# A subtraction on [128, 1024] tiles moved from VectorE to GpSimd

## The chip, the cores and the metric

The kernel runs on one core of one Trainium2 chip. The metric is the device time of one execution in microseconds (us): the median of three runs. A profiled execution stands beside them; its span is the time from the first to the last instruction, and its own time is a little longer than the span.

## The reference

The kernel computes a pooled attention followed by a two-layer block.

```
a      = softmax(phi over the 576 rows)            # 32 memory slots per head
k_m    = a^T k ;  v_m = a^T v                      # 8 batches x 8 heads, 64 wide
attn   = softmax(q k_m^T / 8) ;  out = attn v_m
x      = out, heads side by side                   # 4608 x 512
h      = x @ w_in                                  # 512 x 2048
g      = h - tanh(h)
result = g @ w_out                                 # 2048 x 512, float32
```

The weights arrive as float64.

## The kernel before

Every factor of the two large products is held as two float16 halves, a high half and the remainder (the low half), and three matmuls (high x high, high x low, low x high) stand in for one float32 matmul. The weights become win_hi, win_lo, wout_hi and wout_lo; the attention rows become ah and al; and the product of v_m and w_in becomes ph and pl, so that h comes straight from the attention weights.

The 4608 rows are cut into 18 units of 256, and the 2048 columns of w_in into 4 blocks of 512. A piece of work is a pair (unit, block), written (u, fb), and there are 72 of them. For each pair:

- mm1 (L444): TensorE computes h, four tiles of 128 columns side by side, [128, 1024] float32 in PSUM, from ph, pl, ah and al. ScalarE squares it (L450).
- g1: VectorE multiplies h with its square (L458) into h3, and frees h in PSUM; ScalarE squares u + beta (L459).
- g2: VectorE finishes the value, a polynomial for h - tanh(h), in h3 (L464); ScalarE copies it as float16 into gg[:, 0], the high half (L466).
- g3 (L471): the low half, gg[:, 1] = h3 - gg[:, 0], [128, 1024], float32 minus float16, written as float16. In two of the 72 pairs the difference is made by TensorE and ScalarE instead (L477 to L479).
- mm2 (L498): 24 matmuls with 512 columns add the pair into the two output tiles of its unit. For each output tile eight of them take the high half and four the low half. Where the pair is the last of its sum, the order is high and low of the first output tile, then of the second, so the first low matmul is the ninth; elsewhere both high parts come first, and the first low matmul is the seventeenth.

The tile h3 has two buffers, u two and gg three; h in PSUM has two.

The order of work is in two parts. The first is a list of words written by hand (START), in which all engines get their instructions in the order of the list: the words H, a, b, c and M followed by unit and block stand for mm1, g1, g2, g3 and mm2. It covers units 0 to 3 and the first half of unit 4, and between these words are the loads, the attention of the first batches, and the conversion of the weights from float64. The conversion is done by VectorE with whole-number instructions on [128, 512] (L260, L264, L268), followed by the low half of the weights (L295). The units 0 to 3 are summed in two passes, blocks 0 and 1, then 2 and 3; the partial results go to memory and back, and these DMAs, and the output of those units, are issued by GpSimd (L522). All others are issued by SyncE.

The second part is a regular loop over the rest, one pair to a slot. mm2 of a pair is issued two slots after its mm1. The attention of the batches to come is put between the slots; with it VectorE makes pl from PSUM (L423), transposes scores (L196) and takes maxima, sums and products over them (L205 to L222), and makes al (L399).

Of the kernel before, what the change touches and what calls it, by code (L numbers as in the profile page):

```python
# [14 lines left out]
ALU = mybir.AluOpType  # L15
# [209 lines left out]
def split_path(ctx, tc, c, ins, out):  # L225
    nc = tc.nc
# [241 lines left out]

    def g3(u, fb):
        h3, gg = gs[u, fb]  # L470
        nc.vector.tensor_tensor(gg[:, 1], h3, gg[:, 0], op=ALU.subtract)  # L471

    def g3_pe(u, fb):
        h3, gg = gs[u, fb]
# [52 lines left out]
    def warm(*_):  # L527
# [12 lines left out]
        "N": lambda b: att.norm(b, st[b]), "U": lambda b: att.turn(b, st[b]), "UV": att_turn_v, "W": att_window,  # L540
        "S": lambda b, t: att.scores(b, st[b], t), "A": lambda b, i, j: att.soft1(b, st[b], i, j), "B": lambda b, i, j: att.soft2(b, st[b], i, j), "BH": att_ah, "BL": att_al,
        "Z": warm, "P": att_p, "PL": att_pl, "H": mm1, "a": g1, "b": g2, "c": g3, "d": g3_pe,
        "T": lambda x, y: conv(10 * x + y, False), "E": lambda x, y: conv(10 * x + y, True),
        "L": lambda x, y: low_dve(10 * x + y), "K": lambda x, y: low_pe(10 * x + y),
# [41 lines left out]
    for sl, (u, fb) in enumerate(slots, 18):  # L586
        for f in (mm1, g1, g2, g3):
            f(u, fb)
        queue.append((u, fb))
        for f, x in tasks.get(sl, []):  # L590
            f(x)
        u, fb = queue.pop(0)
        mm2(u, fb, fb == (2 if u in parts else 0), fb == NFB - 1)
        if sl == 68:
            check(tc, c, big, ps_a)
# [210 lines left out]
```

## Time and profile before

| what | value |
|---|---|
| median of three runs | 696.86 us (695.42 to 697.27) |
| profiled execution: its time | 696.4 us |
| profiled execution: span | 694.6 us |
| PE busy | 664.5 us, 96% |
| DVE (VectorE) busy | 477.4 us, 69% |
| ACT (ScalarE) busy | 398.3 us, 57% |
| POOL (GpSimd) busy | 10.8 us, 2% |
| chain that ended last, by engine | PE 78%, DVE 17%, DMA 3%, issue 1%, ACT 1% |
| mean granted clock of TensorE | 0.991 |

In the profile PE is TensorE's matmuls, PEld its weight loads, SP SyncE's queue. L471 is line 471 of the kernel. A row of groups has the line, the engine, the operation, what it writes and reads, the count, then the busy time, the mean duration of one in ns, and the idle time of the engine just before, with what ended it. A row of the timeline has the start, the duration (of all that are merged in the row), and the instruction. A row of the waits says who waited for whom, the total, how often, and the longest. The chain is followed back from the last instruction; its rows have a start, a length, and who held it. A matmul's end is modelled, so what PE really waits for is read from the waits and the chain, not from the busy share.

### The profile page before, as it was taken

What the parts mean: (1) busy time and instruction counts of PE and PEld (TensorE: products, weight loads), DVE (VectorE), ACT (ScalarE), POOL (GpSimd) and SP (SyncE); (2) the same over time, 40 slices, a digit from 0 to 9 for tenths busy, and PEclk for the clock granted to TensorE, in tenths of its full rate; (3) what the DMA queues carried; (4) which work ended last, traced back from release to release, by engine and by line L of the source; (5) the groups of instructions that cost most, each with busy time, mean ns of one, the idle gap of its engine ahead of it and who ended that gap; (6) DMA issues with size and microseconds to landing.
All of it is one profiled execution on the core that took longest, in us unless ns stands there. A gap on an engine that the chain in (4) does not pass through costs nothing.

```text
span 694.6 us, 13671 instructions
## 1 busy us (share of the span) xinstructions
PE 664.5 (96%) x5992; PEld 392.1 (56%) x5992; DVE 477.4 (69%) x571; ACT 398.3 (57%) x526; POOL 10.8 (2%) x26
## 2 busy tenths in 40 slices
PE   2688999999999999999999999999999999999996
PEld 2345574664656556666555655665566555666552
DVE  6699999998976596446596559556955695444541
ACT  3447666664545865665865595556645664544341
POOL 0000000001000000000000000000000000000000
PEclk9799999999999999999999999999999999999999
DMA  9955534682413940002940195009200300000001
GB/s 322 361 200 202 194 130 156 205 278 77 148 62 108 341 130 6 27 16 89 344 131 2 59 361 157 2 32 331 96 1 31 123 32 1 32 1 32 1 30 36
DMA packets 34003, 84.87 MB, mean 122 GB/s; under 512 B 3472, under 2 KB 8208, under 8 KB 33936
## 3 DMA queue, kind: packets, MB, share of 16 engines
q1 hardware_dynamic: 32512, 79.59, 33.3%
q0 software_dynamic: 1280, 4.20, 1.6%
q8 instruction: 49, 0.80, 0.5%
q14 instruction: 18, 0.15, 0.1%
q10 hardware_dynamic: 144, 0.13, 0.1%
HBM read 72.37 MB, written 11.53 MB: 121 GB/s over the span
## 4 chain that ended last, share of the span: by engine, by line
PE 78%; DVE 17%; DMA 3%; issue 1%; ACT 1%; SPq 0%; DVEq 0%
PE o L498 47%; PE h L444 22%; PE pkv L147 3%; PE pp L411 3%; DVE wt L264 2%; DVE wt L268 2%; DVE h L458 2%; DVE h L464 2%; DVE wt L260 1%; DMA kv<-in_kva_dram 1%; PE psc L187 1%; DVE g L471 1%; DVE ph L423 1%; DVE wout_lo L295 1%; DMA chk<-in_w_out_dram 1%
## 5 line engine op out<-in xcount | busy, mean ns | idle before, releaser
L498 PE MATMUL o<-wout_hi,g 128*128 128x512 f16 x1152 | 354.4, 379 | 0.8 <-ACT g L466 0.8
L498 PEld LDWEIGHTS <-g 128*128 128x128 f16 x1728 | 164.2, 98 | 206.9 <-issue 16.7
L498 PE MATMUL o<-wout_lo,g 128*128 128x512 f16 x576 | 218.4, 379 | 0.0
L444 PE MATMUL h<-ah,ph 128*128 128x256 f16 (+3 forms) x1536 | 201.2, 246 | 0.4 <-DVE h L458 0.4
L444 PEld LDWEIGHTS <-ph 128*128 128x128 f16 x2304 | 178.6, 98 | 28.9 <-issue 2.5
L444 PE MATMUL h<-al,ph 128*128 128x256 f16 (+3 forms) x768 | 170.1, 246 | 0.0
L458 DVE SCALAR_TENSOR_TENSOR h<-h,u 128x1024 f32<-128x1024 f32 x72 | 87.5, 1218 | 67.6 <-ACT u L450 67.6
L450 ACT ACTIVATE u<-h 128x1024 f32<-128x1024 f32 x72 | 73.2, 1018 | 91.5 <-PE h L444 91.5
L471 DVE TENSOR_TENSOR g<-h,g 128x1024 f16<-128x1024 f32 x70 | 85.3, 1221 | 49.8 <-ACT g L466 49.8
L466 ACT ACTIVATE g<-h 128x1024 f16<-128x1024 f32 x72 | 76.0, 1056 | 72.9 <-DVE h L464 72.9
L459 ACT ACTIVATE u<-u,beta 128x1024 f32<-128x1024 f32 x72 | 82.6, 1147 | 51.3 <-DVE h L458 50.6
L464 DVE SCALAR_TENSOR_TENSOR h<-u,h 128x1024 f32<-128x1024 f32 x72 | 87.9, 1221 | 25.8 <-ACT u L459 24.5
L423 DVE SCALAR_TENSOR_TENSOR ph<-pp,ph 128x1024 f16<-128x1024 f32 x32 | 38.9, 1216 | 2.4 <-ACT ph L418 2.4
L418 ACT ACTIVATE ph<-pp 128x1024 f16<-128x1024 f32 x32 | 32.5, 1016 | 1.9 <-PE pp L411 1.9
L516 ACT ACTIVATE ot<-o 128x512 f32<-128x512 f32 x35 | 20.5, 588 | 14.3 <-PE o L498 14.2
L147 PE MATMUL pkv<-kv,e 128*32 128x129 f32 (+1 forms) x640 | 25.6, 294 | 2.6 <-DMA kv<-in_kva_dram 2.2
L196 DVE STREAM_TRANSPOSE sc<-psc 128x288 f32<-128x288 f32 x32 | 13.5, 459 | 19.6 <-PE psc L187 19.6
L309 ACT ACTIVATE fy<-chk 128x512 f32<-128x512 f32 x32 | 21.4, 667 | 5.2 <-DMA chk<-in_w_in_dram 2.8
L310 ACT ACTIVATE fy<-fy,one 128x512 f32<-128x512 f32 x32 | 23.0, 719 | 0.7
L147 PEld LDWEIGHTS pkv<-kv,e 128*32 128x32 f32 (+1 forms) x640 | 17.1, 114 | 10.8 <-issue 5.9
L264 DVE SCALAR_TENSOR_TENSOR wt<-raw,wt 128x512 uint32<-128x512 uint32 x32 | 20.7, 688 | 0.0
L268 DVE SCALAR_TENSOR_TENSOR wt<-raw,wt 128x512 uint32<-128x512 uint32 x32 | 20.6, 687 | 0.0
(96 smaller groups left out, 372.3 us busy)
## 6 DMA issues: line engine op xcount, KB each, us to landing
kv<-in_kva_dram SPq DMA_DIRECT2D x32, 516.0 KB, 7.7
q<-in_qt_dram SPq DMA_DIRECT2D x16, 576.0 KB, 7.0
raw<-in_w_in_dram SPq DMA_DIRECT2D x16, 512.0 KB, 6.6
raw<-in_w_out_dram SPq DMA_DIRECT2D x16, 512.0 KB, 5.1
chk<-in_w_in_dram SPq DMA_DIRECT2D x16, 512.0 KB, 5.0
chk<-in_w_out_dram SPq DMA_DIRECT2D x16, 512.0 KB, 5.3
out_dram<-ot SPq DMA_DIRECT2D x27, 256.0 KB, 2.0
pt<-in_phx_dram SPq DMA_DIRECT2D x8, 576.0 KB, 4.4
```

Of the source, the lines that this page charges most:

```text
L147: nc.tensor.matmul(pa[32 * h : 32 * h + 32, r, 0:129], e[0:K, c, 32 * hh : 32 * hh + 32], d["kv"][h][0:K, r, c, :], start=(c == 0), stop=( ...
L264: nc.vector.scalar_tensor_tensor(t, r[:, :, 0], 29, t, op0=ALU.logical_shift_right, op1=ALU.bitwise_or)
L268: nc.vector.scalar_tensor_tensor(t, r[:, :, 1], 0xC0000000, t, op0=ALU.bitwise_and, op1=ALU.bitwise_or)
L423: nc.vector.scalar_tensor_tensor(pl, pa, S_P / (S_V * S_W), ph, op0=ALU.mult, op1=ALU.subtract)
L444: nc.tensor.matmul(hp[:, k, tu : tu + w], px[:, g, cs], d[ax][:, g, ta : ta + w], start=(n == 0), stop=(n == 5),)
L450: nc.scalar.activation(uu, hp, AF.Square, scale=1.0 / (S_A * S_P))
L458: nc.vector.scalar_tensor_tensor(h3, hp, C2 * S_G / (S_A * S_P), uu, op0=ALU.mult, op1=ALU.mult)
L459: nc.scalar.activation(uu, uu, AF.Square, bias=c["beta"])
L464: nc.vector.scalar_tensor_tensor(h3, uu, CC, h3, op0=ALU.add, op1=ALU.mult)
L466: nc.scalar.activation(gg[:, 0], h3, AF.Copy)
L471: nc.vector.tensor_tensor(gg[:, 1], h3, gg[:, 0], op=ALU.subtract)
L498: nc.tensor.matmul(o, gx[:, k, P * tt : P * tt + P], wx[:, 4 * fb + k, :], start=(first and k == 0 and wx is wout_hi and gx is gh), stop=( ...
```

## The change

The subtraction g3 is issued on GpSimd's queue instead of VectorE's. Nothing else in the source is changed; g3 is called 70 times, 16 of them for units 0 to 3 and the first two of unit 4 through the word c, the rest from the loop.

```diff
     def g3(u, fb):
         h3, gg = gs[u, fb]
-        nc.vector.tensor_tensor(gg[:, 1], h3, gg[:, 0], op=ALU.subtract)
+        nc.gpsimd.tensor_tensor(gg[:, 1], h3, gg[:, 0], op=ALU.subtract)
```

On GpSimd's queue, in the hand-ordered part, the subtractions stand between the DMA issues of the partial results. Before (d is a partial result in memory, ot the tile it comes from):

```order
L522 DMA d_808<-ot_806 128x512
L522 DMA d_824<-ot_822 128x512
L522 DMA d_1055<-ot_1053 128x512
L522 DMA d_1071<-ot_1069 128x512
L522 DMA d_1248<-ot_1246 128x512
L522 DMA d_1264<-ot_1262 128x512
```

and now (g_747 belongs to the pair (0,1), g_914 to (1,1), g_1079 to (2,0), g_1092 to (2,1), g_1227 to (3,0), g_1370 to (3,1)):

```order
L471 TENSOR_TENSOR g_747<-h_705,g_747 128x1024
L522 DMA d_808<-ot_806 128x512
L522 DMA d_824<-ot_822 128x512
L471 TENSOR_TENSOR g_914<-h_898,g_914 128x1024
L522 DMA d_1055<-ot_1053 128x512
L522 DMA d_1071<-ot_1069 128x512
L471 TENSOR_TENSOR g_1079<-h_1038,g_1079 128x1024
L471 TENSOR_TENSOR g_1092<-h_1073,g_1092 128x1024
L522 DMA d_1248<-ot_1246 128x512
L522 DMA d_1264<-ot_1262 128x512
L471 TENSOR_TENSOR g_1227<-h_1180,g_1227 128x1024
L471 TENSOR_TENSOR g_1370<-h_1307,g_1370 128x1024
```

The subtraction of (3,0) is behind the two issues of d_1248 and d_1264, each of which waits for ScalarE's output copy.

On VectorE, in the middle of the same part, two subtractions leave a row of instructions that convert weights (wt, win_lo) and finish the pairs (2,0), (2,1) and begin (3,0):

```order
 L295 SCALAR_TENSOR_TENSOR win_lo<-wt_1081,win_hi 128x512
 L295 SCALAR_TENSOR_TENSOR win_lo<-wt_1082,win_hi 128x512
-L471 TENSOR_TENSOR g_1079<-h_1038,g_1079 128x1024
-L471 TENSOR_TENSOR g_1092<-h_1073,g_1092 128x1024
 L458 SCALAR_TENSOR_TENSOR h_1180<-h_1123,u_1148 128x1024
 L260 TENSOR_SCALAR wt_1187<-raw_1150 128x512
```

L458 of (3,0), which writes the h3 buffer that (2,0) had, now follows the weights' low half directly, and has a wait on GpSimd that it did not need while the subtraction was ahead of it on VectorE's own queue.

## The prediction

> **What bounds the kernel now.** I read the windows first, because a busy share over the whole span mixes two stages.
>
> ```profile
> 75.00:155.00 80.00, 79.08 (x750) 48.19 (x748) 79.76 (x111) 50.43 (x67) 5.53 (x8) 1.00 0.59 196
> 155.00:170.00 15.00, 15.00 (x102) 6.27 (x102) 13.52 (x18) 6.92 (x8) 1.08 (x2) 1.00 0.24 80
> 260.00:680.00 420.00, 419.73 (x3754) 250.61 (x3753) 253.09 (x257) 246.27 (x318) 0.00 (x0) 1.00 0.23 80
> ```
>
> The columns after the length are PE, weight loads, DVE, ACT and POOL busy, then the granted clock and the DMA share. From 260 to 680 us PE is busy 419.73 of 420 us at full clock while DVE works 253 us: TensorE is the bound. From 75 to 155 us (the hand-ordered start, from the first subtraction on) DVE is busy 79.76 of 80 us and PE 79.08: both are full. Next, who keeps PE waiting from 75 us on:
>
> ```profile
> PE o L498 <- ACT g L466: 0.8, 1, 0.8
> PE psc L187 <- DVE sc L196: 0.3, 1, 0.3
> PE pp L411 <- DVE e L135: 0.2, 1, 0.2
> ```
>
> That is all: 1.3 us by this table, 1.2 us by the windows (0.92 + 0.27). **So the largest possible gain is 1.2 us**, however much VectorE is relieved; a loss has no such limit. The chain of waits says where a late VectorE would hurt:
>
> ```profile
> 152.62 1.15 DVE h L464
> 153.78 1.07 ACT g L466
> 154.90 5.35 PE o L498 x24
> ```
>
> Ahead of these rows the chain runs through DVE for the whole of the full window, and only here does it pass to PE, where it stays. The second matmul of (0,3) starts as soon as its high half exists. Whatever VectorE loses between 75 and 154 us, PE loses there.
>
> **What is moved.** 70 subtractions:
>
> ```profile
> L471 DVE TENSOR_TENSOR g<-h,g 128x1024 f16<-128x1024 f32 x70 | 85.3, 1221 | 49.8 <-ACT g L466 49.8
> masks.py:199 POOL TENSOR_SCALAR_AFFINE_SELECT ident<-ident 128x128 f32<-128x128 f32 x1 | 0.3, 283 | 0.0
> masks.py:197 POOL MEMSET ident<- 128x128 f32 x1 | 0.2, 204 | 0.3 <-POOLq L795 0.3
> L761 POOL MEMSET one<- 128x1 f32 x1 | 0.1, 88 | 0.0
> ```
>
> On VectorE one takes 1.22 us (1.14 from start to start in a row of instructions). GpSimd has not run it. Its own rows bound it: filling 128x128 takes 204 ns, 128x1 88 ns, so 0.09 us fixed and 0.9 ns per element with no input; the select, with one input, takes 283 ns, so 1.5 ns per element. One input more costs 0.6 ns, so I estimate 2.1 ns with two, and 1024 x 2.1 ns + 0.09 = **2.3 us**. The lower end is VectorE's 1.22, the upper twice the one-input price, 2 x 1.5 x 1.024 + 0.09 = 3.2 us. I take 2.3, since it continues the step between the two GpSimd rows.
>
> The Trainium skill, "GPSIMD Engine Reference", section "Performance versus the Vector engine", has a two-input fp32 add 1.96 times as long on GpSimd; as an estimate that is 1.96 x 1.22 = 2.4 us, which would add about 0.1 us to each term below; no run here shows it yet.
>
> **Do the two engines hold each other up?** This decides the sign. GpSimd's DMA issues beside what VectorE runs at that moment:
>
> ```profile
> 98.79 0.54 POOL L522 DMA_DIRECT2D d<-ot  x1 [16.68 <-ACT ot L516]
> 100.29 0.80 POOL L522 DMA_DIRECT2D d<-ot  x1 [0.96 <-ACT ot L516]
> 116.77 0.54 POOL L522 DMA_DIRECT2D d<-ot  x1 [0.30 <-ACT ot L516]
> 100.21 0.76 DVE L260 TENSOR_SCALAR wt<-raw 128x512 uint32<-128x512 uint32 x2
> 116.26 1.30 DVE L264 SCALAR_TENSOR_TENSOR wt<-raw,wt 128x512 uint32<-128x512 uint32 x2
> ```
>
> Beside L260 an issue takes 0.80 instead of 0.54 us, ending about when L260 ends; beside L264 it stays at 0.54. So GpSimd can be shut out, by L260 at least. An issue does not stream tiles, though, and the subtraction does: L264 may well collide with that. Bounds: nothing held, and each subtraction holding VectorE for its whole 2.3 us. I take as held the VectorE instructions that, like L260, work in SBUF alone (L264, L268, L295, L464), and as free those that read PSUM (L423, L458, L132), because the one collision in the trace is of the first kind.
>
> The Trainium skill, "SBUF — State Buffer", section "Who interferes with whom", says that a VectorE instruction with two SBUF inputs collides with a GpSimd instruction that reads SBUF but not with one that only writes it, and that whoever starts first keeps the other out until it is done. The two issue rows fit: L260 collides, L264 does not collide with an issue. By L260 alone VectorE would come out 5.6 us ahead of now (no gain beyond the 1.2 us), by this rule behind.
>
> **The sum.** When each subtraction can start (the end of its L466), for (0,1), (1,1), (2,0), (2,1), (3,0), (3,1), (0,2), (1,2), (0,3), (1,3):
>
> ```profile
> 73.22 1.06 ACT L466 ACTIVATE g<-h 128x1024 f16<-128x1024 f32 x1 [0.50 <-DVE h L464]
> 89.18 1.06 ACT L466 ACTIVATE g<-h 128x1024 f16<-128x1024 f32 x1 [1.22 <-DVE h L464]
> 100.94 1.05 ACT L466 ACTIVATE g<-h 128x1024 f16<-128x1024 f32 x1
> 104.55 1.06 ACT L466 ACTIVATE g<-h 128x1024 f16<-128x1024 f32 x1 [0.51 <-DVE h L464]
> 113.68 1.05 ACT L466 ACTIVATE g<-h 128x1024 f16<-128x1024 f32 x1
> 125.54 1.05 ACT L466 ACTIVATE g<-h 128x1024 f16<-128x1024 f32 x1
> 137.65 1.06 ACT L466 ACTIVATE g<-h 128x1024 f16<-128x1024 f32 x1 [0.47 <-DVE h L464]
> 142.70 1.06 ACT L466 ACTIVATE g<-h 128x1024 f16<-128x1024 f32 x1 [0.32 <-DVE h L464]
> 153.78 1.06 ACT L466 ACTIVATE g<-h 128x1024 f16<-128x1024 f32 x1 [0.50 <-DVE h L464]
> 165.86 1.06 ACT L466 ACTIVATE g<-h 128x1024 f16<-128x1024 f32 x1 [0.51 <-DVE h L464]
> ```
>
> and what VectorE runs then, one row for each of the first eight:
>
> ```profile
> 74.31 1.21 DVE L423 SCALAR_TENSOR_TENSOR ph<-pp,ph 128x1024 f16<-128x1024 f32 x1
> 90.27 1.22 DVE L423 SCALAR_TENSOR_TENSOR ph<-pp,ph 128x1024 f16<-128x1024 f32 x1
> 102.09 1.29 DVE L268 SCALAR_TENSOR_TENSOR wt<-raw,wt 128x512 uint32<-128x512 uint32 x2
> 107.90 1.22 DVE L458 SCALAR_TENSOR_TENSOR h<-h,u 128x1024 f32<-128x1024 f32 x1
> 117.46 1.30 DVE L268 SCALAR_TENSOR_TENSOR wt<-raw,wt 128x512 uint32<-128x512 uint32 x2
> 126.14 1.22 DVE L132 TENSOR_TENSOR e<-e,pmx 128x1024 f32<-128x1024 f32 x1
> 138.25 1.35 DVE L264 SCALAR_TENSOR_TENSOR wt<-raw,wt 128x512 uint32<-128x512 uint32 x2
> 147.19 2.35 DVE L458 SCALAR_TENSOR_TENSOR h<-h,u 128x1024 f32<-128x1024 f32 x2
> ```
>
> Each entry is the time VectorE is held, less the 1.14 us that it no longer spends. (0,1), (1,1), (2,1): one free instruction runs beside the subtraction, then a held one waits the other 1.15 us: 0 each. (2,0), (0,2): it falls among held instructions, 2.3 - 1.1 = +1.2 each. (3,0): it is queued behind a DMA issue that waits until 116.77 and takes 0.54, so it meets L268 at 117.4: +1.2. (3,1): L132 and the short row behind it end 1.1 us after the start, so 1.2 are held: +0.1. (1,2): with the two subtractions gone L423 and both L458 (147.19) come right after it, all free: -1.1. Together **+2.6 us** at (0,3). h3 has two buffers, so L458 now waits for GpSimd: (3,0)'s, the closest, needs (2,0)'s subtraction, which ends about 105.0, ahead of 105.6 when L458 can start.
>
> Then the low halves themselves. PE's first low matmul stands eight matmuls behind the high one:
>
> ```profile
> 156.64 0.59 PE L498 MATMUL o<-wout_hi,g 128*128 128x512 f16 x2
> 168.71 0.59 PE L498 MATMUL o<-wout_hi,g 128*128 128x512 f16 x2
> 677.74 1.06 ACT L466 ACTIVATE g<-h 128x1024 f16<-128x1024 f32 x1 [1.29 <-DVE h L464]
> 684.87 0.81 PE L498 MATMUL o<-wout_hi,g 128*128 128x512 f16 x3
> ```
>
> For (0,3) that is 156.64 - 154.84 = 1.8 us after ACT, for (1,3) 168.71 - 166.92 = 1.8, and GpSimd needs 2.3 + 0.1 to be seen: **+0.6 us** each. Sum +3.8, if a subtraction gets in after the current VectorE instruction. If instead VectorE goes first until it comes to a PSUM reader, (3,0) becomes -1.1 and (0,2) +0.5, so the entries sum to about -0.4; but (0,3) starts a VectorE instruction (1.1 us) later: some +2.0 in all. No row tells these apart; I take the middle, **+2.9 us**.
>
> From 170 us on I cost the edit at nothing: the second matmul stands two slots behind, and even the last unit, the tightest, has 684.87 - 678.80 = 6.1 us from ACT to first use. VectorE's 40% idle time there takes up the holds; uncovered, 2.3 us a slot would be over 100 us. GpSimd's DMA issues now stand between subtractions up to about 210 us; at 0.54 to 0.80 us each they block little, and what they write is read or ends much later.
>
> The profiled execution has 694.6 us of span and 696.4 us in all; 694.6 + 2.9 = 697.5, with the same 1.8 around it 699.3. The median is 0.46 above that execution, so **699.8 us**.
>
> **Rivals.** (a) *No hold worth the name* (or L260's alone): VectorE gains, at most 8 x 1.14 = 9.1 us by (0,3), both late low halves come early enough, and PE closes its 1.2 us: 695.7. For it: the 0.54 beside L264. Against: 0.80 beside L260. (b) *GpSimd is slower than 2.3 us*, by itself or because VectorE stretches it: at 3.2 us seven of the eight entries grow by 0.9 and the two low halves too, 3.8 + 9 x 0.9 = +11.9, up to 708.8; held half that way, about 704. It outweighs (a)'s gain as soon as an average hold exceeds the 1.14 us saved. For it: VectorE has no gap in 75 to 155 us in which GpSimd would be alone. Against: four of the eight fall on free instructions. (c) *The change does not do what it says*: the order shows 70 rows on GpSimd's queue and none on VectorE's; under 1%.
>
> **How the numbers follow.** 0.3% is 2.1 us, about what a measurement here tells from none. Forecast: 0.50; its own range is +0.2 to +5.6 us (697.1 to 702.5), since 0.2 us more or less than 2.3 moves nine terms, 1.8 us beyond each end. (a) 0.28, (b) 0.21, the rest 0.01. The range reaches from 695.0, (a) with the 0.7 us to spare that the three runs show below, to 706.5, two thirds of (b); under 2 in 10 are left out. Faster by over 2.1 us is beyond the idle time of PE: 0.04. Same: (a) less that, and nearly a third of the forecast, the part of its range up to 2.1: 0.24 + 0.15 = 0.39. Slower: 0.57.
>
> **What would show it.** In the changed profile: L471 on POOL near 2.3 us, longer only beside L260, L264, L268, L295 or L464; those rows with a mean above now's (L264 690 ns); L423 and L458 unchanged; PE waiting at o L498 near 155 us for ACT g, and for POOL g at (0,3) and (1,3); PE from 260 to 680 us still full. If L264 and its like keep their means, (a) holds. If PE waits for POOL after 260 us, my zero there is wrong.

## The result and the profile after

The changed kernel takes 700.66 us (median of four runs, 699.87 to 701.33), the kernel before, run beside it, 696.65 us (695.42 to 697.27). The ratio is **1.0056, 95% interval 1.0034 to 1.0077**: 4.0 us slower. The forecast was 699.8 us, +2.9. Of the later runs of the kernel before, one slow one of 1392.8 us is left out of the ratios.

The same windows as in the prediction, of the changed kernel (after the length: PE, weight loads, DVE, ACT and POOL busy, granted clock, DMA share, GB/s), with 20 to 40 us ahead of them:

```profile
20.00:40.00 20.00, 16.69 (x154) 8.83 (x154) 15.53 (x32) 7.97 (x13) 0.00 (x0) 0.91 0.92 322
75.00:155.00 80.00, 78.22 (x741) 47.49 (x739) 75.23 (x101) 49.24 (x66) 27.30 (x16) 1.00 0.57 191
155.00:170.00 15.00, 13.31 (x94) 5.45 (x95) 11.30 (x17) 7.46 (x9) 7.52 (x5) 1.00 0.25 78
260.00:680.00 420.00, 419.03 (x3751) 250.03 (x3750) 196.93 (x208) 246.70 (x319) 103.60 (x49) 1.00 0.23 80
```

and of the kernel before, the one window not shown yet:

```profile
20.00:40.00 20.00, 15.79 (x151) 8.62 (x152) 14.53 (x30) 6.81 (x10) 0.00 (x0) 0.74 0.93 325
```

Up to the first subtraction at 73 us both kernels run the same instructions, but the granted clock from 20 to 40 us was 0.74 in the one profiled execution and 0.91 in the other, and the changed kernel reaches the second matmul of (0,1) 1.2 us earlier (74.09 against 75.28 us). That is not the change's doing (over the runs below this clock is 0.74 to 1.00), so differences are taken from there on. From 260 to 680 us PE is as full as before but for 0.7 us, though DVE has lost 56 us of work. VectorE is less busy in the start too (75.23 of 80 us, before 79.76), and PE is nevertheless idle longer, above all from 155 to 170 us: 13.31 of 15 us busy instead of 15.00.

Who keeps PE waiting between 75 and 260 us (total, times, longest):

```profile
PE o L498 <- POOL g L471: 2.7, 3, 1.3
PE o L498 <- ACT g L466: 0.8, 1, 0.8
PE o L498 <- DVE wout_lo L295: 0.5, 1, 0.5
```

The first row is new, and it is three waits for the low half. The changed kernel's chain of waits runs through two of them, (3,0) and (1,3):

```profile
116.20 3.74 POOL g L471
...
168.77 2.71 POOL g L471
```

To see where the 4 us arise, I took the moment at which the second matmul of a pair starts, in both traces, and the difference between the two from one pair to the next:

| from | to | lost, us | what |
|---|---|---|---|
| (0,1) | (3,0) | 0.31 | |
| (3,0) | (3,1) | 0.64 | low half of (3,0) late |
| (3,1) | (0,2) | -0.08 | |
| (0,2) | (0,3) | 0.84 | VectorE late, and so the copy of (0,3) |
| (0,3) | (1,2) | 1.44 | low half of (0,3) late |
| (1,2) | (1,3) | -0.07 | |
| (1,3) | (2,2) | 0.94 | low half of (1,3) late |
| (2,2) | (3,3) | 0.00 | |

The sum is 4.0 us, and all of it lies between 75 and 181 us. (The two spans, 694.6 and 698.1 us, differ by 3.5: 4.0, less the 1.2 of the early start, and 0.7 for a wait of the scores for VectorE near 550 us, 1.0 instead of 0.3 us. This wait is 0.7 us in low_later_before below as well, where no subtraction is on GpSimd, and loop_only shows no loss that can be measured.) By PE's own steps three quarters of it, 3.0 us, stand at low halves that come late, and one quarter at other delay of VectorE.

Up to (0,3) the rows are not independent, because there PE waits for the copy in both traces (0.76 us before, 0.77 now). What PE lost ahead of it counts only as far as it made VectorE late:

```profile
124.98 1.22 DVE L132 TENSOR_TENSOR e<-e,pmx 128x1024 f32<-128x1024 f32 x1 [0.72 <-PE pmx L127]
...
146.52 1.23 DVE L423 SCALAR_TENSOR_TENSOR ph<-pp,ph 128x1024 f16<-128x1024 f32 x1 [1.75 <-ACT ph L418]
...
155.42 0.39 PE L498 MATMUL o<-wout_hi,g 128*128 128x512 f16 x1 [0.77 <-ACT g L466]
```

VectorE had come to L132 ahead of the kernel before and lost that lead in 0.72 us of standing for PE's pmx: that is where the 0.64 us of (3,0) went. Counted from (0,1), it starts L132 0.03 us later than before, L458 behind the L260 that the subtraction of (3,1) held 0.87 us later (131.49 against 131.81), and the copy of (0,3) ends 1.72 us later. For the last step, L464 of (1,2) is held by the subtraction of (0,2) (141.14 below), ScalarE's copy of (1,2) waits for it, ScalarE makes ph (L418) only then, and L423 waits 1.75 us for ph. PE's 0.5 us for wout_lo delayed nothing on VectorE's side.

The instructions themselves, groups of the start of the changed kernel, 75 to 160 us:

```profile
L464 DVE SCALAR_TENSOR_TENSOR h<-u,h 128x1024 f32<-128x1024 f32 x10 | 14.3, 1428 | 0.0
L458 DVE SCALAR_TENSOR_TENSOR h<-h,u 128x1024 f32<-128x1024 f32 x10 | 11.9, 1212 | 4.1 <-POOL g L471 4.0
L264 DVE SCALAR_TENSOR_TENSOR wt<-raw,wt 128x512 uint32<-128x512 uint32 x16 | 10.3, 683 | 0.0
...
L260 DVE TENSOR_SCALAR wt<-raw 128x512 uint32<-128x512 uint32 x16 | 9.8, 652 | 0.0
```

Between 75 and 155 us of the kernel before these means were 1217 (L464), 1213 (L458), 690 (L264), 686 (L268) and 422 ns (L260). So L464 and L260 got longer, L264 and L268 (678) did not, and L458 now stands idle 4.0 us in front, waiting for GpSimd to release an h3 buffer.

All 70 subtractions, shortest, median and longest in ns, then the first and last start:

```profile
L471 POOL TENSOR_TENSOR g<-h,g x70: 2124/2131/5368, 73.2 to 682.5; 128x1024 f16<-128x1024 f32 x70
```

What that is in time is seen on the two engines side by side. GpSimd of the changed kernel, its subtractions in the start (start, duration of the row; x2 is two of them):

```profile
73.15 2.13 POOL L471 TENSOR_TENSOR g<-h,g 128x1024 f16<-128x1024 f32 x1 [71.63 <-ACT g L466]
...
100.88 7.47 POOL L471 TENSOR_TENSOR g<-h,g 128x1024 f16<-128x1024 f32 x2 [1.23 <-PE h L444]
116.20 3.73 POOL L471 TENSOR_TENSOR g<-h,g 128x1024 f16<-128x1024 f32 x1
...
138.53 3.96 POOL L471 TENSOR_TENSOR g<-h,g 128x1024 f16<-128x1024 f32 x1 [0.39 <-ACT g L466]
...
155.44 5.18 POOL L471 TENSOR_TENSOR g<-h,g 128x1024 f16<-128x1024 f32 x2 [8.57 <-DMA kv<-in_kvt_dram]
168.77 2.70 POOL L471 TENSOR_TENSOR g<-h,g 128x1024 f16<-128x1024 f32 x1 [4.97 <-ACT g L466]
```

and VectorE of the changed kernel:

```profile
74.24 2.13 DVE L464 SCALAR_TENSOR_TENSOR h<-u,h 128x1024 f32<-128x1024 f32 x1
...
100.64 1.28 DVE L268 SCALAR_TENSOR_TENSOR wt<-raw,wt 128x512 uint32<-128x512 uint32 x2
101.84 1.21 DVE L464 SCALAR_TENSOR_TENSOR h<-u,h 128x1024 f32<-128x1024 f32 x1
102.98 1.28 DVE L295 SCALAR_TENSOR_TENSOR win_lo<-wt,win_hi 128x512 f16<-128x512 f32 x2
106.28 1.22 DVE L458 SCALAR_TENSOR_TENSOR h<-h,u 128x1024 f32<-128x1024 f32 x1 [2.02 <-POOL g L471]
...
116.66 1.27 DVE L268 SCALAR_TENSOR_TENSOR wt<-raw,wt 128x512 uint32<-128x512 uint32 x2
117.86 1.21 DVE L423 SCALAR_TENSOR_TENSOR ph<-pp,ph 128x1024 f16<-128x1024 f32 x1
...
126.45 2.71 DVE L260 TENSOR_SCALAR wt<-raw 128x512 uint32<-128x512 uint32 x2
...
141.14 2.44 DVE L464 SCALAR_TENSOR_TENSOR h<-u,h 128x1024 f32<-128x1024 f32 x1
155.34 1.22 DVE L464 SCALAR_TENSOR_TENSOR h<-u,h 128x1024 f32<-128x1024 f32 x1
```

A subtraction with nothing in its way takes 2.13 us (the median, and the first row). Where GpSimd was first, L464 (74.24, 141.14) or L260 (126.45, two in 2.71 us instead of 0.76) was held until GpSimd was done, and worked then. Where VectorE was first, GpSimd's row is longer by its time outside. The one at 100.88, (2,0), is the longest: 5.37 us, to 106.25 (the rest of the row is (2,1)). Working 2.13 us, it can have got in only at 104.12, where the second L295 is nearly over (102.98 + 1.28 = 104.26): five VectorE instructions, the rest of one L268, another, L464 and two L295, kept it out in succession. The one at 116.20 ended at 119.93, so it got in at 117.80, where the second L268 is nearly over (117.93) and L423, which reads PSUM, comes next. The one at 138.53 likewise got in at 140.36, again at the end of a row of L264 and L268. And L458 at 106.28 waited 2.02 us for the late subtraction of (2,0). (What the rows at 100.88 and 155.44 name in brackets is inferred by the profile; both start as ScalarE's copy of their pair ends, at 100.80 and 155.37.)

### The profile page after: what moved, and what is told of

It reads as the page before. It is cut to its first block, busy times and chain, and to the rows that moved or that the text cites. A ratio compares the mean times of both kernels' runs of the same rounds, so it can differ in the third digit from the quotient of the medians.

```text
span 698.1 us, 13856 instructions
## 1 busy us (share of the span) xinstructions
PE 665.3 (95%) x5992; PEld 391.9 (56%) x5992; DVE 403.7 (58%) x501; ACT 397.9 (57%) x526; POOL 168.6 (24%) x96
## 4 chain that ended last, share of the span: by engine, by line
PE 80%; DMA 6%; DVE 6%; issue 3%; POOL 2%; ACT 1%; SPq 1%; ACTq 0%; POOLq 0%; DVEq 0%
PE o L498 47%; PE h L444 23%; PE pkv L147 3%; DMA raw<-in_w_out_dram 3%; PE pp L411 3%; DMA kv<-in_kva_dram 1%; POOL g L471 1%; PE psc L187 1%; DMA kv<-in_kvt_dram 1%; DVE wt L264 1%; DVE wt L260 1%; DMA chk<-in_w_out_dram 1%; DVE h L458 1%; DVE wt L268 1%; DMA d<-ot 1%
## 5 line engine op out<-in xcount | busy, mean ns | idle before, releaser
L498 PE MATMUL o<-wout_hi,g 128*128 128x512 f16 x1152 | 354.5, 379 | 3.5 <-POOL g L471 2.7
L498 PEld LDWEIGHTS <-g 128*128 128x128 f16 x1728 | 163.9, 98 | 211.2 <-issue 17.8
L471 POOL TENSOR_TENSOR g<-h,g 128x1024 f16<-128x1024 f32 x70 | 157.9, 2258 | 478.8 <-ACT g L466 416.2
L498 PE MATMUL o<-wout_lo,g 128*128 128x512 f16 x576 | 218.4, 379 | 0.5 <-DVE wout_lo L295 0.5
L458 DVE SCALAR_TENSOR_TENSOR h<-h,u 128x1024 f32<-128x1024 f32 x72 | 87.4, 1217 | 152.6 <-ACT u L450 112.6
L464 DVE SCALAR_TENSOR_TENSOR h<-u,h 128x1024 f32<-128x1024 f32 x72 | 90.0, 1250 | 25.1 <-ACT u L459 23.7
L423 DVE SCALAR_TENSOR_TENSOR ph<-pp,ph 128x1024 f16<-128x1024 f32 x32 | 38.9, 1214 | 6.2 <-ACT ph L418 6.2
L418 ACT ACTIVATE ph<-pp 128x1024 f16<-128x1024 f32 x32 | 32.5, 1017 | 2.1 <-PE pp L411 2.1
L264 DVE SCALAR_TENSOR_TENSOR wt<-raw,wt 128x512 uint32<-128x512 uint32 x32 | 20.6, 682 | 0.0
L268 DVE SCALAR_TENSOR_TENSOR wt<-raw,wt 128x512 uint32<-128x512 uint32 x32 | 20.5, 680 | 0.0
```

Source lines behind the costliest of these rows:

```text
L264: nc.vector.scalar_tensor_tensor(t, r[:, :, 0], 29, t, op0=ALU.logical_shift_right, op1=ALU.bitwise_or)
L418: nc.scalar.activation(ph, pa, AF.Copy, scale=sc)
L423: nc.vector.scalar_tensor_tensor(pl, pa, S_P / (S_V * S_W), ph, op0=ALU.mult, op1=ALU.subtract)
L458: nc.vector.scalar_tensor_tensor(h3, hp, C2 * S_G / (S_A * S_P), uu, op0=ALU.mult, op1=ALU.mult)
L464: nc.vector.scalar_tensor_tensor(h3, uu, CC, h3, op0=ALU.add, op1=ALU.mult)
L471: nc.gpsimd.tensor_tensor(gg[:, 1], h3, gg[:, 0], op=ALU.subtract)
```

## Experiments

Ratios are to the kernel before, timed beside it on the same chip. Its medians there were 695.6 us (first four experiments), 695.8 (the two of low_later) and 695.5 (the other three), about 1 us below the first measurement, so an expectation in microseconds is to be read as a difference. Where an edit adds a line, L471 becomes L472 and L498 becomes L499.

**Where in the program is it?** The loop alone, and the start alone:

```diff
-        nc.gpsimd.tensor_tensor(gg[:, 1], h3, gg[:, 0], op=ALU.subtract)
+        eng = nc.gpsimd if (u, fb) >= (4, 2) else nc.vector      # loop_only
+        eng = nc.gpsimd if (u, fb) < (4, 2) else nc.vector       # start_only
+        eng.tensor_tensor(gg[:, 1], h3, gg[:, 0], op=ALU.subtract)
```

> Only the 54 subtractions of the regular loop are on GpSimd; the 16 of the hand-ordered start stay on VectorE. Theory (the loss of 4.0 us is made in the start, between 110 and 172 us, where the two engines keep each other out): the time is that of the kernel before, 696.7 +- 0.7 us, and TensorE waits for GpSimd nowhere. Rival (part of it is lost in the loop, where TensorE's wait for the transposed scores near 550 us grew from 0.3 to 1.0 us): 697.4 to 699.

> Only the 16 subtractions of the hand-ordered start are on GpSimd; the 54 of the loop stay on VectorE. Theory: all of the loss is there, 700.0 to 701.3 us, with TensorE waiting for GpSimd three times, 2.7 us together, at (3,0), (0,3) and (1,3). Rival (the loop's share): 0.7 us or more less than with all 70, 698 to 700.

The loop alone: 696.18 us, ratio 1.0007 (0.9993 to 1.0021), and PE waits for GpSimd nowhere. The start alone: 698.89 us, ratio 1.0057 (1.0035 to 1.0079), which is the whole loss. PE's waits are those of the full change:

```profile
PE o L499 <- POOL g L472: 2.7, 3, 1.3
```

**Which pairs?** GpSimd for (3,0), (0,2), (0,3) and (1,3) only, and for all but these:

```diff
+        eng = nc.gpsimd if (u, fb) in ((3, 0), (0, 2), (0, 3), (1, 3)) else nc.vector      # four_only
+        eng = nc.gpsimd if (u, fb) not in ((3, 0), (0, 2), (0, 3), (1, 3)) else nc.vector  # four_back
```

> Only the subtractions of (3,0), (0,2), (0,3) and (1,3) are on GpSimd. Theory (these four carry the loss, by the lateness of their own low halves and by what VectorE is held up beside them): TensorE again waits for GpSimd at (3,0), (0,3) and (1,3), and the time is 3 to 5 us above the kernel before, 699.7 to 701.7. Rival (the loss is VectorE's backlog, added up over all of the start): with four of sixteen moved, 1 us or less above it, up to 697.7.

> All but these four, (3,0), (0,2), (0,3) and (1,3), are on GpSimd. Theory: TensorE waits for GpSimd nowhere and VectorE is still relieved of 66 subtractions, so the time is at or just below the kernel before, 695.5 to 697. Rival (backlog over all of the start): 699 or more.

The four alone: 698.98 us, ratio 1.0052 (1.0034 to 1.0070). The other 66: 695.11 us, 0.9998 (0.9982 to 1.0013), without a wait for GpSimd on PE. So four of the 70 subtractions carry the loss, the rest cost nothing that can be told, and freeing VectorE of 66 gained nothing that can be told. The four were not tried one by one. Nor do they do quite the same as in the full change: with the four alone PE waits the same 2.7 us for GpSimd, but 0.8 us for kvn (L161) instead of 0.5 for wout_lo.

**What could be gained?** No subtraction on any engine; the third matmul reads the high half a second time, so the number of matmuls stays:

```diff
     def g3(u, fb):
         h3, gg = gs[u, fb]
-        nc.gpsimd.tensor_tensor(gg[:, 1], h3, gg[:, 0], op=ALU.subtract)
+        pass
@@
-        gh, gl = gg[:, 0], gg[:, 1]
+        gh, gl = gg[:, 0], gg[:, 0]
```

> The 70 subtractions are left out altogether, and the third matmul reads the high half again in place of the low one, so that TensorE does the same work (the low half of the activations is missing from the sum). This is a relief of VectorE with no GpSimd at all. My bound (TensorE has 1.2 us to gain after 75 us): 695.0 to 696.5. Rival (VectorE's load costs TensorE more than its listed waits show): 694 or less.

694.85 us, ratio 0.9993 (0.9979 to 1.0008). Taking all 85 us of them from VectorE gains 0.5 us, and the interval (1.5 us gained to 0.6 lost) agrees with the bound of 1.2 us. In its trace the second matmuls after (0,3) come 1.3 us earlier, counted from (0,1), and at the end 1.4.

**Is it the wait for h3?** L458 of the changed kernel waits twice 2.0 us for GpSimd to release an h3 buffer. With three buffers instead of two (RING holds the same number for the loads that use these buffers):

```diff
-    RING = {"gg": 3, "h3": 2, "uu": 2}
+    RING = {"gg": 3, "h3": 3, "uu": 2}
@@
-        h3 = big.tile([P, 4, UT], F32, tag="h3", name=f"h3{u}{fb}")
+        h3 = big.tile([P, 4, UT], F32, tag="h3", name=f"h3{u}{fb}", bufs=3)
```

> The changed kernel with three buffers for h3 instead of two, so that L458 of the pair after next need not wait for GpSimd's subtraction (two waits of 2.0 us in the changed kernel, at (3,0) and after (0,3)). Theory (the late low halves themselves are the loss, and those two waits fall into time that VectorE has to spare by then): less than 1 us better than the changed kernel, 699.7 to 700.7. Rival (the buffer is what makes VectorE late): back to 697 to 698.5.

699.80 us, ratio 1.0071 (1.0053 to 1.0089). The loss stays, and PE's waits for GpSimd still sum to 2.7 us. Taking away the buffer's wait alone returns nothing.

**Is it where the low half is first used?** With both high parts first in units 0 to 3 the first low matmul is the seventeenth instead of the ninth, in the changed kernel and, as a control, in the kernel before:

```diff
-        order = [(0, both), (0, low), (1, both), (1, low)] if last else [(0, both), (1, both), (0, low), (1, low)]
+        order = [(0, both), (0, low), (1, both), (1, low)] if last and u >= 4 else [(0, both), (1, both), (0, low), (1, low)]
```

> The changed kernel, with the second matmul's order turned for units 0 to 3: where a pair is the last of its sum, both high parts come first and then both low ones, so that the first low matmul is the seventeenth instead of the ninth and comes 1.7 us later at (0,3) and (1,3). Theory (the late low half is what TensorE waits for, about 1.4 us at (0,3) and 0.9 us at (1,3)): those two waits for GpSimd go, the one at (3,0), whose order is as it was, stays at about 0.5 us, and the time falls by about 2.3 us, to 1.002 to 1.003 times the kernel before (697 to 698). Rival (VectorE's backlog is the loss): no better than the changed kernel, 1.005 times or more.

> The same turned order in the kernel before, with all subtractions on VectorE, to see what the order does by itself. Both theories: nothing that can be told, 0.998 to 1.001 times the kernel before, since TensorE waited for no subtraction there.

In the changed kernel 699.00 us, ratio 1.0045 (1.0028 to 1.0061); in the kernel before 695.38 us, 0.9999 (0.9984 to 1.0014). PE's wait for GpSimd falls from 2.7 to 0.7 us, as it should. But the time falls by 0.0011 (from 1.0056), about a third of what was expected, and the two intervals overlap. The waits of low_later, 75 to 260 us:

```profile
PE o L498 <- POOL g L471: 0.7, 1, 0.7
PE psc L187 <- DVE vl L378: 0.8, 1, 0.8
```

The second row is new, and low_later's chain of waits tells where it comes from:

```profile
157.65 3.12 POOL g L471
...
160.79 1.24 DVE h L458
...
162.05 1.15 ACT u L459
163.20 0.17 ACT vh L377
...
163.39 0.30 DVE vl L378
...
163.83 0.72 PE psc L187 x16
```

The late subtraction of (0,3) holds an h3 buffer, L458 waits for it, ScalarE has u behind that and vh behind u, and the scores of the attention wait for vl. In this trace the 0.94 us at (1,3) is gone, but of the 1.44 us at (0,3) 0.91 remain. One late subtraction has two readers, PE and the buffer; taking off the first shows the second. A further 0.46 us is lost near 256 us, where PE waits for ph (L423). The turned order and the third buffer were not tried together.

**How much room has the loop?** Each loop subtraction done twice on GpSimd, the start on VectorE:

```diff
+        if (u, fb) >= (4, 2):
+            nc.gpsimd.tensor_tensor(gg[:, 1], h3, gg[:, 0], op=ALU.subtract)
+            nc.gpsimd.tensor_tensor(gg[:, 1], h3, gg[:, 0], op=ALU.subtract)
+        else:
+            nc.vector.tensor_tensor(gg[:, 1], h3, gg[:, 0], op=ALU.subtract)
```

> As with the loop alone on GpSimd, but each subtraction of the loop is done twice there, one after the other, so that 4.3 us stand between ScalarE's copy and the low half. Theory (the loop has 6.1 us or more from the copy to the first use): the time of the kernel before, 696.7 +- 0.7 us. If the loop's slack is less than I read: a wait for GpSimd in many of 54 slots, 700 or more.

702.36 us, ratio 1.0090 (1.0056 to 1.0125): the expectation missed. PE still never waits for the low half, but for something else:

```profile
PE pp L411 <- DVE ph L423: 5.7, 3, 2.2
```

One of the three places, in loop_twice's timeline (L472 and L473 are the two subtractions):

```profile
353.89 2.13 POOL L472 TENSOR_TENSOR g<-h,g 128x1024 f16<-128x1024 f32 x1 [5.20 <-ACT g L466]
354.90 4.34 DVE L399 SCALAR_TENSOR_TENSOR al<-af,ah 128x576 f16<-128x576 f32 x2 [0.95 <-ACT ah L393]
356.10 2.52 POOL L473 TENSOR_TENSOR g<-h,g 128x1024 f16<-128x1024 f32 x1
```

The same place of loop_only:

```profile
351.36 2.40 DVE L399 SCALAR_TENSOR_TENSOR al<-af,ah 128x576 f16<-128x576 f32 x2 [0.95 <-ACT ah L393]
```

Undisturbed the two L399 take 1.42 us. With one subtraction per pair one of them is held (2.40 us for the two); with two subtractions both are (4.34). L423 is behind L399 on VectorE, and the next pp has only one PSUM buffer, so PE stands for up to 2.2 us, at three places.

**The disputed cost by itself.** A small kernel that computes nothing of the reference: six equal VectorE instructions alone, then with one subtraction released on GpSimd inside the run, then with the subtraction started first. The forms are two inputs in SBUF (like L464), PSUM and SBUF (like L458), one input in SBUF, and L260's form. The lines are cut; all are issued on VectorE.

```python
scalar_tensor_tensor(ys[i], x, 0.5, z, op0=ALU.mult, op1=ALU.add)       # L64: two SBUF inputs
scalar_tensor_tensor(ys[i], hpf, 0.5, z, op0=ALU.mult, op1=ALU.add)     # L67: PSUM and SBUF
tensor_reduce(ms[i], x.rearrange("p (n k) -> p n k", k=32), ...)        # L70: one SBUF input
tensor_scalar(ys[i][:, 0:512].bitcast(U32), wide[:, :, 1], 3, ...)      # L73: L260's form
```

> Not this computation: the output is filled with zeros, and all the rest is left out. GpSimd's subtraction on the kernel's shapes runs alone, then released about 1 us after a run of six VectorE instructions began, then released about 1 us before such a run; the six are of four kinds: two SBUF inputs, one PSUM and one SBUF input, one SBUF input (a maximum), and L260's whole-number form. Theory (exclusion, whoever comes first): alone 2.13 us; behind a run with two SBUF inputs, and behind one of L260's form, it ends only 2.1 us after the run's end (about 8 us for the first), and ahead of such a run the first VectorE instruction is about 1 us longer; with a PSUM input or one SBUF input neither is longer. Rival (the two share, each slowed): GpSimd at 3 to 4 us in the middle of the run and each of the VectorE instructions beside it longer by a part.

```profile
21.75 6.89 DVE L64 SCALAR_TENSOR_TENSOR y<-x,z 128x1024 f32<-128x1024 f32 x6
30.79 8.82 DVE L64 SCALAR_TENSOR_TENSOR y<-x,z 128x1024 f32<-128x1024 f32 x6
31.77 2.20 POOL L81 TENSOR_TENSOR gl<-tb,gh 128x1024 f16<-128x1024 f32 x1 [11.21 <-ACT tb L78]
...
52.86 6.87 DVE L67 SCALAR_TENSOR_TENSOR y<-hp,z 128x1024 f32<-128x1024 f32 x6
61.93 6.87 DVE L67 SCALAR_TENSOR_TENSOR y<-hp,z 128x1024 f32<-128x1024 f32 x6
62.91 2.13 POOL L81 TENSOR_TENSOR gl<-tb,gh 128x1024 f16<-128x1024 f32 x1 [19.01 <-ACT tb L78]
...
106.59 2.10 DVE L73 TENSOR_SCALAR y<-wide 128x512 uint32<-128x512 uint32 x6
110.89 4.02 DVE L73 TENSOR_SCALAR y<-wide 128x512 uint32<-128x512 uint32 x6
```

Six instructions with two SBUF inputs take 6.89 us alone and 8.82 with a subtraction released among them: one of them is longer, by 1.93 us of GpSimd's 2.13. The readers of PSUM take 6.87 with and without, and the reduction, with one input in SBUF, 6.84 always. L260's form goes from 2.10 to 4.02. With the subtraction started first the six take 7.91 and 3.11 us, longer by what was left of it. So the exclusion is there, and it concerns L464's form and L260's, as the prediction had assumed. Its line between the classes, "in SBUF alone", is too wide: the reduction works in SBUF alone and is not held. The Trainium skill, "SBUF — State Buffer", section "Who interferes with whom", says that a VectorE instruction with two SBUF inputs collides with a GpSimd instruction that reads SBUF, and that whoever issues first has the shared pair of ports for its whole instruction. These rows agree. L260 has one SBUF input, so that it collides is shown here by its own rows. The expectation failed in one point: GpSimd was not kept out until the end of the run, it got in behind the instruction that was running.

**Who keeps whom out, and for how long?** In the kernel VectorE kept GpSimd out through three to five instructions in succession, and in that small kernel through one. Two more such kernels looked for the difference: runs of twelve with four release times and three forms (L64's form, L264's on separate tiles, L264's on two tiles in turn),

```python
for op in (two_sbuf, bits, chain):
    for size in (256, 512, 768, 1024):       # a longer copy on ScalarE releases GpSimd later
        ...
        for i in range(12):
            op(i % 6)
        nc.scalar.activation(tb[:, 0:size], ta[:, 0:size], AF.Copy)
        sub(tb)
```

and no, one or two DMA issues ahead of the subtraction on GpSimd, beside an idle VectorE, beside the kernel's own row (two L264, two L268, L464, two L295, twice), and beside a run of twelve:

```python
for run in (none, kernel_like, twelve):
    for dmas in (0, 1, 2):
        for size in (256, 1024):
            ...
            run()
            for k in range(dmas):
                nc.gpsimd.dma_start(parts[k], ta[:, 512 * k : 512 * k + 512])
            nc.scalar.activation(tb[:, 0:size], ta[:, 0:size], AF.Copy)
            sub(tb)
```

> Not this computation: the output is filled with zeros, and all the rest is left out. Twelve VectorE instructions with two SBUF inputs in a row (of 1024 float32; of 512 whole numbers as L264; and the last in place, each on the tile of the one before the last), with one subtraction on GpSimd released at four different times within the run. In the changed kernel the subtraction of (2,0) was kept out through five such VectorE instructions and that of (0,2) through three, yet in the first probe it got in after one. Theory A (GpSimd gets in at the end of the VectorE instruction that is running): a duration of 2.1 us and the rest of that one, 2.1 to 3.3 us (2.1 to 2.8 with 512 elements), and one VectorE instruction longer by 2 us in each run. Theory B (VectorE keeps the access as long as its instructions follow one another, and GpSimd gets in only where it asks just as one ends): mostly the rest of the run and 2.1 us, 8 us and more with 1024 elements, 4 us and more with 512, and no VectorE instruction longer.

> Not this computation: the output is filled with zeros, and all the rest is left out. In the changed kernel the three subtractions that VectorE kept out through several instructions, (2,0), (3,0) and (0,2), are those that follow a DMA issue on GpSimd by 0 to 1.3 us; (0,3), (1,3) and (3,2), with none before them, waited for one VectorE instruction. Here the subtraction comes with no, one or two DMA issues (128x512) ahead of it on GpSimd, beside an idle VectorE, beside a run in the kernel's own order (L264, L268, L464, L295, twice), and beside twelve with two SBUF inputs; released 0.4 or 1 us after the run's start. Theory (a DMA issue just before makes GpSimd lose its turn): with an idle VectorE 2.1 us with and without issues; with a run and no issue 2.1 to 3.3 us; with a run and one or two issues 3.7 us and more. Rival 1 (the kernel's own mix of instructions does it): over 3.5 us also with no issue beside the run in the kernel's order. Rival 2 (GpSimd is still at work on the issue): over 3.5 us also beside an idle VectorE.

In the first, GpSimd's row within a run lasts 2.13 to 3.20 us whatever the form and the moment; the longest:

```profile
67.72 3.20 POOL L81 TENSOR_TENSOR gl<-tb,gh 128x1024 f16<-128x1024 f32 x1 [14.91 <-ACT tb L112]
```

3.20 - 2.13 = 1.07 us is less than one VectorE instruction of 1.14. In the second it is the same: with two issues ahead beside the kernel-like row 2.13 us, beside the run of twelve 2.13 to 3.20 with or without issues:

```profile
147.81 3.20 POOL L90 TENSOR_TENSOR gl<-tb,gh 128x1024 f16<-128x1024 f32 x1 [15.62 <-ACT tb L147]
```

So neither the forms, nor the moment of the release, nor the DMA issues ahead, nor this row of instructions is what lets VectorE go on before GpSimd in the kernel. Nor is DMA traffic: the row at 31.77 of the first small kernel, 2.20 us, lay in a stretch with a DMA share of 1.02, while from 100 to 106 us of the changed kernel the share is 0.62. TensorE does nothing in the small kernels, and that difference was not tried. **That stays open.** It is no accident of one execution: start_only has the same lengths as the full change, 5.4 us at (2,0) and 3.73 at (3,0). In four_only, where VectorE's rows stand otherwise, (0,2) took 2.17 us, with the next L264 held, and (3,0) 3.42; so in the kernel, too, GpSimd can get in between two instructions of a row.

## Why the prediction was right, and where not

- **The gain is bounded by 1.2 us.** Right: no_sub leaves the subtraction out and gains 0.5 us.
- **A subtraction takes 2.3 us.** 2.13 us measured, alone and in the kernel wherever nothing kept it out. The estimate from the two GpSimd rows was 0.17 too long, of which 0.06 is rounding: 1024 x 2.1 ns + 0.09 us are 2.24. The Trainium skill, "GPSIMD Engine Reference", section "Performance versus the Vector engine", gives 1.96 times VectorE's time for an fp32 add; here it is 2.13 / 1.22 = 1.75 times.
- **Which VectorE instructions collide.** Right for L464 and L260 and for the free ones: L458 stays at 1212 ns beside 1213. For L264, L268 and L295 the sign that I named, a longer mean, did not come (683 beside 690 ns). They are of the colliding class all the same; in the kernel they were the ones that were first, and in the last small kernel two of L264's form took 3.21 instead of 1.28 us. So the last test that I gave, rival (a) if L264 keeps its mean, was a bad one: an instruction that goes first keeps its mean too.
- **VectorE comes 2.6 us late to (0,3), or goes first and comes 0.4 early; middle taken.** The middle is 1.1 us. Counted from (0,1) on, the copy of (0,3) is 1.7 us later than before (155.37 against 154.84 us, after a start 1.2 us earlier; 0.31 + 0.64 - 0.08 + 0.84 in the table), so this term was 0.6 too small. It is also not a mean of one mechanism: GpSimd was first at (0,1) and (3,1), VectorE at (2,0), (3,0) and (0,2). The entry of (3,1), priced at +0.1, was 0.8 us: L132 was over when its subtraction began, so L260 was held almost from its start (1.95 us longer, less the 1.14 saved). Being first saved VectorE nothing where its next instruction was L458 of (3,0): h3 came free only at 106.25, and it stood idle 2.02 us. The working had this wait as harmless, with (2,0)'s subtraction ending about 105.0. Since h3_three returns no time, that wait is not the cause of the loss by itself.
- **The low halves of (0,3) and (1,3) are late, 0.6 us each, the first up to 1.1 more.** Right in place and kind, but this is the step that failed most. With the middle of the 1.1 it made 1.75 us; measured were 1.44 + 0.94 = 2.4. The price of 0.6 assumed that GpSimd starts at once. At (0,3) the copy ended at 155.37 us and L464 had started at 155.34: GpSimd got in at 156.4. I had that wait only as the case in which VectorE goes first everywhere, and took half of it. At (1,3) L221, with two SBUF inputs, kept it out, and its row has 2.70 us instead of 2.13; that was not in the working:

```profile
168.72 0.76 DVE L221 TENSOR_TENSOR sc<-sc,sz 128x576 f32<-128x576 f32 x1
```

- **Not in the sum:** the low half of (3,0). Pushed back by DMA issues until 116.20 and by VectorE until 117.80, it cost 0.64 us, which is part of the 1.7 above, since VectorE waited for PE behind it. I had asked what the late (3,0) does to VectorE, and not whether its own reader would wait. And wout_lo, late on VectorE behind L464 (held, 2.44 us), kept PE waiting for 0.5 us, though in time that PE would have stood for the copy of (0,3) anyway.
- **Zero in the loop.** Right (loop_only 1.0007), for a reason that I had only half. The 6.1 us from the copy to the first use are real, and PE never waits for the low half even with two subtractions per pair. But the room of the loop is not that: it is the line on VectorE from L399 to L423 to the next pp, and loop_twice used it up at 5.7 us of waits. Nor does VectorE's idle time have many holds to take up: of its larger groups from 215 to 690 us only L399 got longer, by 2.9 us in all (before, ten of 750 ns; L464 has 1222 ns beside 1223):

```profile
L399 DVE SCALAR_TENSOR_TENSOR al<-af,ah 128x576 f16<-128x576 f32 x10 | 10.0, 1044 | 2.9 <-ACT ah L393 2.9
```

- **The rivals.** "No hold worth the name" is excluded by L464 at 2.13 and 2.44 us, "slower than 2.3 us" by 2.13 us alone; stretched by VectorE it was, in six of the 16 rows of the start (2.70 to 5.37 us). "Does not do what it says": 70 rows on POOL, none on DVE.

So +2.9 stands against +4.0: 1.1 + 1.75 forecast, 1.7 + 2.3 measured (2.4 less 0.07 between them). The sign, the place and the mechanism hold; the price of a late low half was too small, and one late low half was overlooked. That the two numbers lie so near is in part luck: by the prediction's own rule of nine terms, 2.13 in place of 2.3 us takes off 9 x 0.17 = 1.5 us, and the same working then gives +1.4. The subtraction that was priced too long made up for waits that were priced too low or left out.

## What to carry to other kernels

Relieving an engine is worth at most the time that the bounding engine waits for it; here that was 1.2 us beside 85 us of moved work, so the question was only what the move costs. Work that goes to GpSimd is not beside VectorE but in turn with it wherever VectorE has two inputs in SBUF (or an instruction of L260's form), and the delay must be priced at each reader of the moved result: the next product, and the buffer that it keeps. Moving back four pairs out of 70 took the loss away: three whose low half had a reader close behind, and (0,2), whose subtraction held VectorE.

## What the runs showed of the hardware

- GpSimd and VectorE exclude each other for a whole instruction: six instructions take 8.82 us instead of 6.89 when one subtraction of 2.13 us is let in, and not at all longer when one of the two inputs is in PSUM (6.87 us) or in a reduction with one SBUF input (6.84).
- L260, one whole-number input at a step of 8 bytes, is excluded as well: one instruction of 0.42 us became 2.35 in the small kernel, and two in a row took 2.71 instead of 0.76 at 126.45 us of the changed kernel. The collision seen in the trace before, 0.80 instead of 0.54 us of a DMA issue, stood beside an instruction of this form.
- The duration of a GpSimd row here includes the time in which it was kept out, 5.37 us for work of 2.13.
- In this kernel VectorE kept GpSimd out through up to five instructions in succession; in three small kernels, and once in four_only, GpSimd got in after the one that was running. Why is open.
